# Softmax-feature attention and SwiGLU: queries on 128 partitions, score columns in token order, one store for 256 tokens

## Chip, cores, metric

One Trainium2 chip; the kernel runs on one core. The metric is device time of one execution in microseconds. It was measured in 4 runs; another execution was taken by the hardware profiler.

## What is computed

Attention over 32 feature columns instead of 576 keys, in 8 batches of 8 heads, then a SwiGLU block over the 4608 tokens:

```python
batch, n_heads, seq, head_dim, n_mem = 8, 8, 576, 64, 32
a = exp(phi - max(phi, axis=2)); a = a / (sum(a, axis=2) + 1e-9)   # over the sequence
k_m = einsum('bhsm,bhsd->bhmd', a, k)
v_m = einsum('bhsm,bhsd->bhmd', a, v)
scores = 1 / sqrt(64) * matmul(q, k_m.transpose(0, 1, 3, 2))      # 576 x 32 a head
attn = softmax(scores, axis=-1)
x = matmul(attn, v_m).transpose(0, 2, 1, 3).reshape(4608, 512)
out = (silu(x @ w_gate) * (x @ w_val)) @ w_out                     # 512 -> 1536 -> 512
```

Inputs and the output are float32; the kernel works in bfloat16 with float32 sums.

## The kernel before

**Layout of queries.** The loads of q (`load_q_group`, line 104, for batches 0 to 2 in two halves by head parity; `load_q`, line 113, for the others and for batch 3) put 96 partitions of 6 consecutive tokens a head into SBUF, cast to bfloat16, so a DMA row is 6 x 64 floats, 1536 B. Batches 0 to 2 are turned on TensorE (`q_T`, line 375): per call two heads, 6 transposes of 96 x 128, one copy out of PSUM; four calls make a batch, the first two for the heads g = 0, the others for g = 1. Batches 3 to 7 are turned by a transposing DMA on the SP queue (`load_qT`, line 118). A transposed block holds two of a head's token places (r = 0 and 1) in its two halves of 64 partitions.

**Scores and softmax.** `scores(b, g)` (line 400) makes 8 products into two PSUM banks, one for r = 0 and one for r = 1 with 288 score columns each, 32 rows a head; four heads fill the 128 partitions. An exponential on ScalarE (line 415) for each bank writes t_E. For batches 0 and 1 the sum over features is a product with a block of ones, a logarithm and an exponential (`z_inv`, line 421); for the others VectorE makes it (`z_inv_v`, line 434). `norm` (line 453) multiplies. The keys' and values' feature sums come before them (`k_items`, `v_direct`; `kv_items` from batch 2 on), and they are multiplied into the weights (`u_round`, line 463, into t_U), so that no x is formed.

**Gate and value.** `gv_slot` (line 548): for each block of 128 hidden units and each r, two products into p_g, a silu on ScalarE (t_sg), two products into p_v and a multiplication on VectorE into t_h, columns r x 288 onward.

**Output product.** `products` (line 701) makes the output of 512 of a batch's 576 tokens with seven block products instead of eight, of 6 units each (a unit is two matmuls of 256 columns); sums of blocks of t_h (`chunk_done`, line 589) are made ahead on GpSimd and VectorE. The last 64 columns of four batches are gathered in `xs` by a GpSimd copy (`ends`, line 594) and done together (`quad_sums`, line 649, and `leftover`, line 798). Products of one batch are the fillers in the next batch's softmax: `take(n)` hands out n units of `backlog`, and `spread` mixes the rest among the gate slots.

**Token order.** A column of t_h is not a token: places of 96 columns belong to one of the 6 tokens of a partition, in an order by r. So 128 columns of output are cut by `token_segments` (line 682), and `store` (line 692) issues one DMA per segment, two for 128 columns, four for a tile of 256; rows lie 6 tokens apart in the output.

**Order.** The engines' order is written out by hand: lines 937 to 972 are the start (batches 0 and 1, with `warm` products between), 975 to 991 their gate slots, and the loop at line 1016 the other batches. Loads with a cast go through the GpSimd queue, stores through SP; at the end a few go through ACT.

Of the kernel before, what the change touches and what calls it, by code (L numbers as in the profile page):

```python
# [14 lines left out]
def kernel(  # L15
# [23 lines left out]
    B, H, S, D = q.shape  # L39
    M = phi.shape[3]  # L40
    DM, DF = moe_w_gate.shape
    P, J = 96, 6
    JK = 9
    NG = 2
    NP = H // 2
# [15 lines left out]

    ctx.enter_context(tc.manual_schedule())

    out_r = out.rearrange("(b p j) c -> b j p c", b=B, p=P, j=J)


    phis, kvs, qs, qTs = {}, {}, {}, {}
# [33 lines left out]
    def load_v(b):  # L101
        nc.gpsimd.dma_start(out=kvs[b][:, 1], in_=head_pairs(v[b]))

    def load_q_group(b, g):

        if g == 0:
            qs[b] = inp.tile([P, NG, NP, J * D], BF16, tag=f"q{Q_SLOT[b]}", bufs=1, name="t_q")
        nc.gpsimd.dma_start(
            out=qs[b][:, g],
            in_=q[b].rearrange("(i g) (p j) d -> g p i (j d)", g=NG, p=P)[g],  # L110
        )

    def load_q(b):
        t = inp.tile([P, H, J * D], BF16, tag=f"q{Q_SLOT[b]}", bufs=1, name="t_q")
        nc.gpsimd.dma_start(out=t, in_=q[b].rearrange("h (p j) d -> p h (j d)", p=P))
        qs[b] = t

    def load_qT(b):

        t = att.tile([128, H, 3, P], BF16, tag="qT", name="t_qT")  # L120
        nc.sync.dma_start_transpose(
            out=t.rearrange("p h j t -> p (h j) t"),
            in_=qs[b].rearrange("p h f -> p (h f)"),
        )
        for i in range(NP):
            qTs[b, i] = t[:, 2 * i:2 * i + 2].rearrange("p h j t -> p h (j t)")

    W = {}

# [242 lines left out]
        done(p)  # L372
        scaled.add(b)

    def q_T(b, g, n, eng="v"):


        pq = bank([128, 2, HALF], BF16, "p_q")
        for i in range(2):
            for jj in range(3):  # L380
                nc.tensor.transpose(  # L381
                    pq[:, i, P * jj:P * (jj + 1)],
                    qs[b][:, g, 2 * n + i, 2 * D * jj:2 * D * (jj + 1)],
                    ident[0:P, 0:P],
                )
        if g == 0 and n == 0:
            box["qT"] = att.tile([128, H, 3, P], BF16, tag="qT", name="t_qT")
            for i in range(NP):
                qTs[b, i] = box["qT"][:, 2 * i:2 * i + 2].rearrange("p h j t -> p h (j t)")
        t = box["qT"].rearrange("p (i g) j t -> p g i (j t)", g=NG)[:, g, 2 * n:2 * n + 2]  # L390
        if eng == "a":
            nc.scalar.copy(out=t, in_=pq)
        else:
            nc.vector.tensor_copy(out=t, in_=pq)
        done(pq)

    def gv_banks():
# [2 lines left out]
    def scores(b, g):  # L400
        p = gv_banks()
        for i in range(NP):
            for r in range(2):
                nc.tensor.matmul(  # L404
                    p[r][32 * i:32 * i + 32, 0:HALF],
                    lhsT=kTs[b][64 * r:64 * r + 64, g, 32 * i:32 * i + 32],
                    rhs=qTs[b, i][64 * r:64 * r + 64, g],
                    start=True,
                    stop=True,
                    tile_position=(64 * r, 32 * i),  # L410
                )
        e = att.tile([128, 2, HALF], BF16, tag=f"E{g}", name="t_E")
        for r in range(2):
            scale = rks[b][:, g:g + 1] if b in rks else sm_scale
            nc.scalar.activation(out=e[:, r], in_=p[r][:, 0:HALF], func=AF.Exp, scale=scale)
        done(*p)
        es[b, g] = e

# [165 lines left out]
    def blocks(b, c):  # L584

        x = hts[b, c].rearrange("p (m e) t -> p e m t", e=2)
        return [x[:, e, :, 256 * n:256 * n + 256] for n in range(2) for e in range(2)]

    def chunk_done(b, c):

        if b % 2 == 0 and c == 0:
            xs[b // 2] = hpool.tile([128, NJF, 2, 64], BF16, tag="xs", name="t_x")

        def ends():
            nc.gpsimd.tensor_copy(
                out=xs[b // 2][:, 4 * c:4 * c + 4, b % 2], in_=hts[b, c][:, :, S - 64:S]
            )
# [12 lines left out]

        end = c + 1 == NCH
        fourth = b in (3, 7)
        if (b, c) in ((0, 2), (1, 1), (1, 2)):
            late.append(lambda *part: sums(nc.gpsimd if b else nc.vector, *part))
        elif b < 2:
            sums(nc.gpsimd)
        elif end:
            sums(nc.vector)
            if b + 1 == B:
                second.pop()(nc.vector, (2, 3))  # L620
                wait_for(Ss[b, 1][0:1, 3, 0, 0:1])
            else:
                wait_for(t[0:1, 3, 0, 0:1])
                second.pop()(nc.gpsimd, (3, 2))
        else:
            if c:
                sums(nc.gpsimd, (0, 1))
                second.append(sums)
            else:
                sums(nc.gpsimd)  # L630
        if end and b > 1 and not fourth:
            late.append(ends)
        else:
# [15 lines left out]
    def quad_sums(qd):  # L649
# [22 lines left out]
                    subtract(nc.gpsimd, t[:, 2], A12, t[:, 1])  # L672

    beside_sums = {
        (0, 0): lambda: (load_phi(3, nc.gpsimd), load_q_group(2, 0)),
        (1, 0): lambda: (load_q_group(2, 1), load_q(3)),
        (0, 1): lambda: (load_k(3), load_v(3)),
    }

    turn = [1]  # L680

    def token_segments(b, t0, count):
        segs = []
        t = t0
        while t < t0 + count:
            blk, pp = divmod(t, P)
            n = min(P - pp, t0 + count - t)
            segs.append((t - t0, n, b, 2 * (blk % 3) + blk // 3, pp))
            t += n
        return segs  # L690

    def store(t_o, b, t0, count, row=0, cols=slice(0, 512), queues=None):

        for r0, m, bb, jj, pp in token_segments(b, t0, count):
            eng = nc.sync
            if queues:
                turn[0] += 1
                eng = queues[turn[0] % len(queues)]
            eng.dma_start(out=out_r[bb, jj, pp:pp + m, cols], in_=t_o[row + r0:row + r0 + m])

    def products(b, by_hand, quad=None):

# [6 lines left out]
        def A(e, n):  # L709
            if quad is not None:  # L710
                return lambda c, m, u: xs[2 * quad + n][:, 4 * c + 2 * m + e].rearrange(
                    "p a t -> p (a t)"
                )
            return lambda c, m, u: hts[b, c][
                :, 2 * m + e, 256 * n + 128 * u:256 * n + 128 * u + 128
            ]

        def Sx(n):
# [52 lines left out]
                done(mine[home])  # L771

        def both(name, t0, cols):
            for u in range(U):
                store(mine[name][:, u, cols], b, t0 + 128 * u, 128, cols=cols)

        def c11():
            t = tile_of("o1", (128, 2, DM), tag="to")
# [17 lines left out]
            both("o2", 256, slice(0, DM))  # L796

        def leftover(name, room, half, cols):
            queues = dict(c22=(nc.scalar,), c21=(nc.scalar, nc.sync)).get(name) if end else None

            def run():
                if room:
# [12 lines left out]
                    done(home)  # L815
                for k in range(2):
                    x = 4 * quad + 2 * (name > "c20") + k
                    store(t, x, S - 64, 64, 64 * k, cols, queues)

            return run  # L820

# [18 lines left out]
        return first + five + six + three + seven + four, ops  # L840

    def q_items(b, evac):
        return [
            lambda g=g, n=n: q_T(b, g, n, evac[2 * g + n]) for g in range(NG) for n in range(2)
        ]

    def u_item(b, c, evac="avav"):

# [51 lines left out]
    load_phi(1, nc.scalar)  # L900
    exp_tables()
    load_k(0)
    for g in range(NG):
        load_q_group(0, g)
    load_k(1)
    nc.vector.memset(bones, 0.0)
    nc.vector.memset(ones1, 1.0)
# [6 lines left out]
    for b in range(2):  # L914
        phi_zeros(b, nc.vector)
        phi_exp_masked(b)
    for g in range(NG):
        load_q_group(1, g)
    load_v(0)
    load_v(1)  # L920
    for half in range(2):
# [14 lines left out]

    warm(104)
    k0, k1 = k_items(0, "vvvv"), k_items(1, "vvvv")
    q0, q1 = q_items(0, "vvvv"), q_items(1, "vvvv")
    run(k0)  # L940
    warm(8)
    run(k1[:1])
    warm(4)
    run(q0[:2])
    warm(2)
    scores(0, 0)
    run(q0[2:])
    warm(2)
    z_inv(0, 0)
    scores(0, 1)  # L950
# [1 line left out]
    run(k1[1:])  # L952
    warm(3)
    z_inv(0, 1)
    run(q1[:2])
    warm(2)
    scores(1, 0)
    norm(0, 0)
    run(q1[2:])
    norm(0, 1)  # L960
    warm(3)
    z_inv(1, 0)
# [175 lines left out]
```

## Time and profile before

| | us |
|---|---|
| median of 4 runs (236.79 to 237.23) | 236.99 |
| profiled execution | 236.76 |
| its span, first to last instruction | 235.0 |

| engine | busy us | share of the span |
|---|---|---|
| TensorE products (PE) | 225.2 | 96% |
| TensorE weight loads (PEld) | 170.4 | 73% |
| VectorE (DVE) | 185.2 | 79% |
| ScalarE (ACT) | 173.0 | 74% |
| GpSimd (POOL) | 144.0 | 61% |

PE's products overlap in the records, so a full PE row means that products follow one another without a gap. SP only issues DMAs. The granted TensorE clock is 1.000 over the span. DMA engines are over 90% busy from about 6 to 70 us and less from then on, save in single slices. Times in the profile's lines are from the start of the span; a line of a timeline shows the start, the duration, the engine, the line of the kernel, the operation, out<-in and how many instructions it stands for.

### The profile page before, as it was taken

The page shows a single profiled execution, that of the slowest core. Times are in us where ns is not written, and L with a number is a line of the kernel's source. Part 1 is how long each engine was busy: PE and PEld are TensorE (multiplying, and loading weights), DVE is VectorE, ACT ScalarE, POOL GpSimd, SP SyncE. Part 2 cuts the span into 40 slices and gives each one's busy share as a digit, 9 for nine tenths or more (in the row PEclk, how much of TensorE's full clock was granted, in tenths as well). Part 3 has the DMA queues.
Part 4 walks back from the last instruction along what each step waited for, and adds up shares of the span by engine and source line. Part 5 has one row for each costly group of instructions (what it writes and reads, how often), then busy time and mean ns, then how long its engine had stood idle before and what let it go on. Part 6 is the DMA issues. An engine that isn't in the chain of part 4 may idle for free.

```text
span 235.0 us, 7317 instructions
## 1 busy us (share of the span) xinstructions
PE 225.2 (96%) x2842; PEld 170.4 (73%) x2842; DVE 185.2 (79%) x425; ACT 173.0 (74%) x368; POOL 144.0 (61%) x193
## 2 busy tenths in 40 slices
PE   7998899999998999999999999999999999999992
PEld 2555467778886677877788787887788778878881
DVE  4157799999976797999798667998799879977732
ACT  2758889987447888968896658978898789677220
POOL 8542427999099069664976689464845494039390
PEclk9999999999999999999999999999999999999999
DMA  6999999999996991999199945999022803212125
GB/s 210 203 205 207 197 207 206 227 239 250 207 196 170 256 217 22 273 219 181 35 198 246 236 128 86 247 229 119 7 85 75 141 0 93 59 46 76 42 62 167
DMA packets 42594, 36.84 MB, mean 157 GB/s; under 512 B 15424, under 2 KB 37952, under 8 KB 42560
## 3 DMA queue, kind: packets, MB, share of 16 engines
q0 software_dynamic: 21440, 22.42, 54.5%
q1 hardware_dynamic: 20352, 13.18, 25.3%
q10 hardware_dynamic: 768, 0.79, 1.0%
q8 instruction: 22, 0.36, 0.6%
q14 instruction: 12, 0.10, 0.1%
HBM read 42.47 MB, written 9.44 MB: 221 GB/s over the span
## 4 chain that ended last, share of the span: by engine, by line
PE 86%; DMA 10%; DVE 1%; issue 1%; ACT 0%; POOLq 0%
PE p_v L518 21%; PE p_g L518 21%; PE p_os L739 20%; PE p_oc L739 10%; DMA W<-in_moe_w_gate_dram 7%; PE p_oa L739 5%; PE p_u L475 5%; DMA t_kv<-in_k_dram 3%; PE p_kv L234 2%; PE p_g L404 1%; PE p_q L381 0%; DVE t_bkv L270 0%; DVE t_U L499 0%; PE p_kv L262 0%; ACT t_U L497 0%
## 5 line engine op out<-in xcount | busy, mean ns | idle before, releaser
L541 DVE TENSOR_TENSOR t_h<-t_sg,p_v 128x288 bf16<-128x288 bf16 x192 | 82.3, 451 | 17.7 <-PE p_v L518 7.7
L518 PEld LDWEIGHTS <-t_U 128*128 128x128 bf16 x768 | 73.7, 98 | 23.7 <-issue 3.2
L535 ACT ACTIVATE t_sg<-p_g 128x288 bf16<-128x288 f32 x192 | 74.4, 423 | 18.6 <-PE p_g L518 11.9
L518 PE MATMUL p_g<-t_A,t_U 128*128 128x288 bf16 x384 | 77.2, 286 | 1.3 <-DVE t_U L499 0.7
L518 PE MATMUL p_v<-t_A,t_U 128*128 128x288 bf16 x384 | 77.2, 286 | 0.0
L739 PEld LDWEIGHTS <-t_S 128*128 128x128 bf16 x384 | 37.4, 98 | 4.5 <-issue 0.2
L605 POOL TENSOR_TENSOR t_S<-t_h 128x512 bf16<-128x512 bf16 x17 | 19.6, 1155 | 31.3 <-DVE t_h L541 29.6
L739 PEld LDWEIGHTS <-t_h 128*128 128x128 bf16 x288 | 26.9, 98 | 8.9 <-issue 5.3
L495 ACT CAST t_U<-p_u 128x512 bf16<-128x512 f32 x53 | 28.0, 607 | 6.9 <-PE p_u L475 6.9
L739 PE MATMUL p_os<-t_T,t_S 128*128 128x256 bf16 x192 | 23.7, 273 | 0.0
L563 POOL TENSOR_TENSOR t_S<-t_S,t_h 128x512 bf16<-128x512 bf16 x17 | 19.6, 1155 | 1.3
L563 POOL TENSOR_TENSOR t_S<-t_h 128x512 bf16<-128x512 bf16 x16 | 18.4, 1150 | 0.0
L563 POOL TENSOR_TENSOR t_S<-t_h,t_S 128x512 bf16<-128x512 bf16 x16 | 18.4, 1150 | 0.0
L475 PE MATMUL p_u<-W,t_kT 64*32 64x512 bf16 (+1 forms) x416 | 15.8, 364 | 0.4 <-DMA W<-in_moe_w_gate_dram 0.4
L739 PE MATMUL p_os<-t_T,t_h 128*128 128x256 bf16 x96 | 15.3, 274 | 0.0
L889 PE MATMUL p_warm<-bones 128*128 128x512 bf16 (+2 forms) x43 | 12.9, 429 | 1.7 <-DVE bones L912 1.7
L499 DVE CAST t_U<-p_u 128x512 bf16<-128x512 f32 x19 | 12.4, 682 | 2.0 <-PE p_u L475 2.0
L739 PE MATMUL p_oc<-t_T,t_S 128*128 128x256 bf16 x96 | 12.0, 273 | 0.0
L739 PE MATMUL p_oa<-WO,t_h 128*128 128x256 bf16 x96 | 11.8, 273 | 0.0
L739 PE MATMUL p_oc<-WO,t_S 128*128 128x256 bf16 x96 | 11.8, 272 | 0.0
L739 PE MATMUL p_os<-WO,t_h 128*128 128x256 bf16 x96 | 11.8, 272 | 0.0
L455 DVE TENSOR_TENSOR t_A<-t_E,t_lz 128x576 bf16<-128x576 bf16 x16 | 11.4, 739 | 0.3 <-ACT t_lz L431 0.3
(107 smaller groups left out, 314.8 us busy)
## 6 DMA issues: line engine op xcount, KB each, us to landing
t_kv<-in_k_dram POOLq DMA_DIRECT2D x8, 576.0 KB, 11.3
t_kv<-in_v_dram POOLq DMA_DIRECT2D x8, 576.0 KB, 14.9
out_dram<-t_o SPq DMA_DIRECT2D x23, 192.0 KB, 2.7
t_phi<-in_phi_dram POOLq DMA_DIRECT2D x6, 576.0 KB, 10.1
t_q<-in_q_dram POOLq DMA_DIRECT2D x5, 576.0 KB, 8.9
out_dram<-t_o SPq DMA_DIRECT2D x31, 64.0 KB, 2.3
out_dram<-t_o SPq DMA_DIRECT2D x14, 128.0 KB, 3.6
t_q<-in_q_dram POOLq DMA_DIRECT2D x6, 288.0 KB, 11.5
```

What stands on the lines that cost most here:

```text
L234: nc.tensor.matmul(p[g][32 * i:32 * i + 32, 0:n], lhsT=phi_of(b, g, j, i), rhs=kvs[b][64 * g:64 * g + 64, w0:w1, i, j * D:(j + 1) * D], st ...
L455: nc.vector.tensor_tensor(out=a, in0=es.pop((b, g)), in1=lzs.pop((b, g)), op=ALU.mult)
L475: nc.tensor.matmul(p[g][32 * i:32 * i + 32, o:o + n], lhsT=kTs[b][64 * g:64 * g + 64, 2, 32 * i:32 * i + 32], rhs=w_part(w, c, i, g, halve ...
L495: nc.scalar.copy(out=t, in_=p)
L499: nc.vector.tensor_copy(out=t, in_=p)
L518: nc.tensor.matmul(p[:, 0:HALF], lhsT=Us[b, c, g][:, o // 2, which, 128 * (o % 2):128 * (o % 2 + 1)], rhs=atts[b, g][:, r], start=(g == 0) ...
L535: nc.scalar.activation(out=sg, in_=gate[:, 0:HALF], func=AF.Silu)
L541: nc.vector.tensor_tensor(out=dst, in0=sg, in1=val[:, 0:HALF], op=ALU.mult)
L563: eng.tensor_tensor(out=out, in0=x, in1=y, op=ALU.subtract)
L605: eng.tensor_tensor(out=t[:, 0], in0=A21, in1=A22, op=ALU.add)
L739: nc.tensor.matmul(mine[home][:, u], lhsT=lhs(c, m, u), rhs=rhs(c, m), start=fresh and u == 0, stop=(k == 5), skip_group_check=u == 1 or n ...
L889: nc.tensor.matmul(p[:, 0:128 * a], lhsT=bones, rhs=x.to_broadcast([128, a, 128]) if a > 1 else bones, start=True, stop=True,)
```

## The change

- q of a batch is one load on 128 partitions, each with 36 consecutive rows of the (head, token) matrix: 16 partitions a head, 9216 B a partition. The halves of `load_q_group` are gone, and batch 2's whole q is loaded where its first half was.
- A batch has 18 transposed blocks of 128 x 128 instead of 24 of 96 x 128. A block holds two row places of every head. On TensorE: three calls of 6 transposes with one copy of 768 columns each, instead of four with 576. In the start all three stand before the first scores of the batch. Batch 2's copies are all on ScalarE.
- `scores` reads its moving operand as 18 runs of 16 columns, 128 apart (`q_of`).
- The exponential reads its bank in another order (18 columns, 16 apart, then the next 18) and so writes columns in token order: column t of half r is token 2t + r.
- Blocks of the output product start at columns 0 and 288 instead of 0 and 256, so the left-over columns are the last 32 of each half; the GpSimd copy that gathers them interleaves them to tokens 512 to 575.
- A tile of 256 tokens is one DMA with rows two tokens apart; a left-over tile is two stores of consecutive tokens. At the end these go one on SP and one on ACT, save the first product's. The segments are gone.
- The last product of batch 1 (six units) runs before the gate slots of batch 2 instead of as a backlog among them.

```diff
-    P, J = 96, 6
+    NS, NC = 18, 16
...
-    out_r = out.rearrange("(b p j) c -> b j p c", b=B, p=P, j=J)
+    out_b = out.rearrange("(b t) c -> b t c", b=B)
+    out_r = out.rearrange("(b t r) c -> b r t c", b=B, r=2)
...
-    def load_q_group(b, g):
...
+    def load_q(b):
+
+        t = inp.tile([128, NS * 128], BF16, tag=f"q{Q_SLOT[b]}", bufs=1, name="t_q")
         nc.gpsimd.dma_start(
-            out=qs[b][:, g],
-            in_=q[b].rearrange("(i g) (p j) d -> g p i (j d)", g=NG, p=P)[g],
+            out=t,
+            in_=q[b].rearrange("h s d -> (h s d)").rearrange("(p f) -> p f", p=128),
         )
...
     def load_qT(b):
 
-        t = att.tile([128, H, 3, P], BF16, tag="qT", name="t_qT")
...
+        qTs[b] = att.tile([128, NS, 128], BF16, tag="qT", name="t_qT")
+        nc.sync.dma_start_transpose(out=qTs[b], in_=qs[b])
+
+    def q_of(b, i, g, r):
+
+        h = NG * i + g
+        return qTs[b][64 * r:64 * r + 64, :, NC * h:NC * h + NC]
...
+    def q_T(b, n, eng="v"):
+
+        k = NS // 3
+        pq = bank([128, k, 128], BF16, "p_q")
+        for x in range(k):
+            y = k * n + x
+            nc.tensor.transpose(pq[:, x], qs[b][:, 128 * y:128 * y + 128], ident)
+        if n == 0:
+            qTs[b] = att.tile([128, NS, 128], BF16, tag="qT", name="t_qT")
+        copy(eng, qTs[b][:, k * n:k * n + k], pq)
         done(pq)
...
-                    rhs=qTs[b, i][64 * r:64 * r + 64, g],
+                    rhs=q_of(b, i, g, r),
...
-            nc.scalar.activation(out=e[:, r], in_=p[r][:, 0:HALF], func=AF.Exp, scale=scale)
+            nc.scalar.activation(
+                out=e[:, r].rearrange("p (c s) -> p c s", c=NC),
+                in_=p[r][:, 0:HALF].rearrange("p (s c) -> p c s", c=NC),
+                func=AF.Exp,
+                scale=scale,
+            )
...
-        return [x[:, e, :, 256 * n:256 * n + 256] for n in range(2) for e in range(2)]
+        return [x[:, e, :, HALF * n:HALF * n + 256] for n in range(2) for e in range(2)]
...
             nc.gpsimd.tensor_copy(
-                out=xs[b // 2][:, 4 * c:4 * c + 4, b % 2], in_=hts[b, c][:, :, S - 64:S]
+                out=xs[b // 2][:, 4 * c:4 * c + 4, b % 2].rearrange("p o (t r) -> p o t r", r=2),
+                in_=hts[b, c].rearrange("p o (r t) -> p o t r", r=2)[:, :, 256:],
             )
...
-        (0, 0): lambda: (load_phi(3, nc.gpsimd), load_q_group(2, 0)),
-        (1, 0): lambda: (load_q_group(2, 1), load_q(3)),
+        (0, 0): lambda: (load_phi(3, nc.gpsimd), load_q(2)),
+        (1, 0): lambda: load_q(3),
...
+    def store_block(t_o, b, n, cols):
+
+        nc.sync.dma_start(
+            out=out_r[b, n, 0:256, cols].rearrange("(u t) c -> t u c", u=2), in_=t_o[:, :, cols]
+        )
+
+    def store_leftover(t_o, b, cols, eng):
+
+        eng.dma_start(out=out_b[b, 512:S, cols], in_=t_o)
...
-                :, 2 * m + e, 256 * n + 128 * u:256 * n + 128 * u + 128
+                :, 2 * m + e, HALF * n + 128 * u:HALF * n + 128 * u + 128
...
-            for u in range(U):
-                store(mine[name][:, u, cols], b, t0 + 128 * u, 128, cols=cols)
+            store_block(mine[name], b, t0 // 256, cols)
...
-            queues = dict(c22=(nc.scalar,), c21=(nc.scalar, nc.sync)).get(name) if end else None
+            engs = (nc.sync, nc.scalar if end and name != "c11" else nc.sync)
...
-                    store(t, x, S - 64, 64, 64 * k, cols, queues)
+                    store_leftover(t[64 * k:64 * k + 64], x, cols, engs[k])
...
-    q0, q1 = q_items(0, "vvvv"), q_items(1, "vvvv")
+    q0, q1 = q_items(0, "vvv"), q_items(1, "vvv")
...
-    run(q0[:2])
+    run(q0)
     warm(2)
     scores(0, 0)
-    run(q0[2:])
...
-    run(q1[:2])
+    run(q1)
     warm(2)
     scores(1, 0)
     norm(0, 0)
-    run(q1[2:])
...
-            kv, q2 = kv_items(2), q_items(2, "aava")
+            kv, q2 = kv_items(2), q_items(2, "aaa")
...
-            backlog = one[36:]
+            run(one[36:])
```

More of the change, by code (lines that the diff above doesn't have):

```diff
@@ L102, in load_v @@
         nc.gpsimd.dma_start(out=kvs[b][:, 1], in_=head_pairs(v[b]))
-    def load_q_group(b, g):
-        if g == 0:
-            qs[b] = inp.tile([P, NG, NP, J * D], BF16, tag=f"q{Q_SLOT[b]}", bufs=1, name="t_q")
+    def load_q(b):
+        t = inp.tile([128, NS * 128], BF16, tag=f"q{Q_SLOT[b]}", bufs=1, name="t_q")
         nc.gpsimd.dma_start(
-            out=qs[b][:, g],
-            in_=q[b].rearrange("(i g) (p j) d -> g p i (j d)", g=NG, p=P)[g],
-        )
-    def load_q(b):
-        t = inp.tile([P, H, J * D], BF16, tag=f"q{Q_SLOT[b]}", bufs=1, name="t_q")
-        nc.gpsimd.dma_start(out=t, in_=q[b].rearrange("h (p j) d -> p h (j d)", p=P))
+            out=t,
+            in_=q[b].rearrange("h s d -> (h s d)").rearrange("(p f) -> p f", p=128),
+        )
         qs[b] = t
     def load_qT(b):
-        t = att.tile([128, H, 3, P], BF16, tag="qT", name="t_qT")
[L121 to L126, printed above, removed]
+        qTs[b] = att.tile([128, NS, 128], BF16, tag="qT", name="t_qT")
[3 more added lines that the diff above has]
+        return qTs[b][64 * r:64 * r + 64, :, NC * h:NC * h + NC]
     W = {}
@@ L373, in v_direct @@
         scaled.add(b)
[L375 to L394, printed above, removed]
+    def q_T(b, n, eng="v"):
[7 more added lines that the diff above has]
+        copy(eng, qTs[b][:, k * n:k * n + k], pq)
         done(pq)
@@ L674 @@
     beside_sums = {
-        (0, 0): lambda: (load_phi(3, nc.gpsimd), load_q_group(2, 0)),
-        (1, 0): lambda: (load_q_group(2, 1), load_q(3)),
+        (0, 0): lambda: (load_phi(3, nc.gpsimd), load_q(2)),
+        (1, 0): lambda: load_q(3),
         (0, 1): lambda: (load_k(3), load_v(3)),
     }
[L680 to L699, printed above, removed]
+    def store_block(t_o, b, n, cols):
[4 more added lines that the diff above has]
+        eng.dma_start(out=out_b[b, 512:S, cols], in_=t_o)
     def products(b, by_hand, quad=None):
@@ L842, in q_items @@
     def q_items(b, evac):
-        return [
-            lambda g=g, n=n: q_T(b, g, n, evac[2 * g + n]) for g in range(NG) for n in range(2)
-        ]
+        return [lambda n=n: q_T(b, n, evac[n]) for n in range(3)]
     def u_item(b, c, evac="avav"):
@@ L902 @@
     load_k(0)
-    for g in range(NG):
-        load_q_group(0, g)
+    load_q(0)
     load_k(1)
@@ L916 @@
         phi_exp_masked(b)
-    for g in range(NG):
-        load_q_group(1, g)
+    load_q(1)
     load_v(0)
```

## The prediction

> **What bounds the kernel now.** I read the page first (the chain of work that ended last), then the chain in order of time, then busy time by stretches, then the timelines of the three places where the chain leaves TensorE.
>
> ```profile
> PE 86%; DMA 10%; DVE 1%; issue 1%; ACT 0%; POOLq 0%
> ```
>
> TensorE (PE) sets the end for 86% of the span. The rest is in these pieces (start us, us, what):
>
> ```profile
> 1.25 8.11 DMA t_kv<-in_k_dram
> 9.64 16.16 DMA W<-in_moe_w_gate_dram
> 25.94 0.37 PE p_u L475 x8
> 26.83 1.15 PE p_g L518 x8
> ...
> 75.53 0.48 issue
> 76.00 0.70 DVE t_U L499
> 76.75 0.54 PE p_g L518 x3
> ...
> 230.50 0.42 DVE t_q L337
> ```
>
> So there are a start of 26.8 us, a hole before the gate products of batch 2, and a tail of 235.0 - 230.9 = 4.1 us after the last copy. Between them PE is full. In the stretches below (length, then PE, PEld, DVE, ACT, POOL busy) PE works 15.40 of 15.40 us:
>
> ```profile
> 76.70:93.00 16.30, 16.25 (x240) 11.97 (x241) 12.95 (x31) 13.72 (x34) 8.71 (x10) 1.00 0.85 174
> 101.60:117.00 15.40, 15.40 (x224) 11.50 (x222) 12.91 (x31) 12.64 (x31) 11.63 (x15) 1.00 0.85 136
> ```
>
> The change neither adds nor removes a product of the MLP. It can move the end only through the start, the hole, the tail, or a slower instruction on the path. I take them in that order, against the profiled execution: 236.76 us (span 235.0 and 1.76 around it), 0.23 below the median of 236.99.
>
> **The start: two chains that end together.** The chain names the load of W. But the other inputs of the first gate product come no earlier (start us, us, engine, what):
>
> ```profile
> 12.70 0.67 PE L381 MATMUL p_q<-ident,t_q 96*128 96x96 bf16 x12
> 13.15 0.82 DVE L394 COPY t_qT<-p_q 128x576 bf16<-128x576 bf16 x2 [0.36 <-PE p_q L381]
> 14.37 0.50 ACT L415 ACTIVATE t_E<-p_g,t_rk 128x288 bf16<-128x288 f32 x1 [3.80 <-PE p_v L404]
> 18.43 0.82 DVE L394 COPY t_qT<-p_q 128x576 bf16<-128x576 bf16 x2
> 19.65 0.50 ACT L415 ACTIVATE t_E<-p_g,t_rk 128x288 bf16<-128x288 f32 x1 [0.41 <-PE p_v L404]
> 24.50 1.28 ACT L967 ACT_TABLE_LOAD   x1
> 25.31 0.98 DVE L337 CAST t_kT<-p_mT 64x64 bf16<-64x64 f32 x4
> 26.33 0.88 DVE L501 TENSOR_SCALAR t_U<-p_u,t_rS 128x256 bf16<-128x256 f32 x2
> ```
>
> W lands at 9.64 + 16.16 = 25.80. The casts of the values' transpose end at 26.29 and the DVE goes on to t_U at once: no slack there. ACT's table load ends at 25.78, its t_U begins at 26.30: slack 0.52.
>
> *The loads get shorter.* The loads land one after the other. k and v (512 rows of 2304 B) land 2.6 to 2.8 us after the load before them. q takes 1.49 + 1.50 for batch 0 and 1.45 + 2.45 for batch 1, in 768 rows of 1536 B. With 128 rows of 9216 B, I give each q the 2.7 us of k: 0.3 and 1.2 saved. W then lands 0.3 to 1.5 earlier, around 24.9. It is worth this only if nothing else is late.
>
> *The scores wait for more.* Now a copy of one half of a head group lets its scores start; then every score column needs all 18 transposed blocks, because each block holds every head. Before: 12 transposes go in 13.21 - 12.70 = 0.51 us, 42.5 ns for 96 columns, so 57 ns for 128. Six of them are done 0.34 us after the start instead of 0.26, so the first copy starts at 13.15 + 0.08 = 13.23. A copy of 576 takes 451 ns and one of 384 takes 349 ns, so 768 should take 553. Three, each overlapping the one before by the 0.08 of the pair above, end at 13.23 + 1.66 - 0.16 = 14.73. The second four score products of group 0 start 0.06 after the copies now (14.03 against 13.97); then at 14.79, 0.76 later. Softmax of batch 0 follows ACT's order, 0.76 late throughout. The transposes of batch 1 (17.83) are behind its sums on PE: 18.59. Their copies come behind the casts of t_kT on the DVE (end 18.40, then 19.16) and take 1.50 to 20.66; scores at 20.72 against 19.31, where the second four stand now. That is 1.41 late. ACT's own chain is only 0.76 late there and so doesn't set it. From t_E at 19.65 to the last sum and the table load nothing waits for DMA, so the table load ends at 27.2, the last normalisation is 1.4 late, behind it on the DVE the casts and t_U, and the first gate product comes at 28.2 instead of 26.83. W, landed by 25, waits. Term: **+1.4 us**. Bounds: -1.5, if the chain has slack that I overlook and the loads gate with their whole gain; +1.6, if the third copy doesn't overlap.
>
> **The hole before batch 2.** The six remaining units of the last product of batch 1 (12 matmuls at 1.31 us per 12, by the chain) run before the gates instead of among them. PE is idle for 0.33 and 0.69 us there, between 75.30 and 76.75; t_U ends at 76.68 whatever PE does. So 1.31 us go into the hole, and the later stretch has 1.31 less. Against this: the copy that ends this product (0.6 us on ACT) now stands before the first silus, and the six units were what PE did while ACT and DVE emptied six banks. Without them PE work there is 16.25 - 1.31 = 14.9 against 13.7 on ACT. Bounds -1.3 (all gained) and 0 (all given back as waits); no row decides, I take the middle: **-0.65**.
>
> **The tail.** The stores of batch 7 and of the leftover tokens pile up on SP:
>
> ```profile
> 230.65 1.76 SPq L699 DMA_DIRECT2D out_dram<-t_q  x3
> 231.00 0.48 ACTq L699 DMA_DIRECT2D out_dram<-t_q  x1
> 227.23 1.92 POOL L563 TENSOR_TENSOR t_Q<-t_x,t_Q 128x256 bf16<-128x256 bf16 x3
> ```
>
> SP's third issue comes at 231.89 and lands 2.1 us later, 233.99; ACT's at 231.00 lands at 233.6. One store for 256 tokens takes six issues of some 0.44 us off SP just before, and the last products then put one store on each queue. The last issue would be at 231.0 on both, landing at 233.1 to 233.6. Bounds 0 (DMA engines are already 0.82 to 0.84 busy from 231 to 233, so bytes may set it) and -0.9; middle **-0.4**. The order of SP's other work is unchanged: the transposes of later q (3.3 to 5.9 us each there) get 18 blocks instead of 24, and land today far ahead of the scores.
>
> **GpSimd's copy of the last 64 tokens** reads pairs 576 B apart instead of runs of 64. Today 419 ns for 256 elements, 24 times, beside PE and 39% idle time of its own. It matters once, at the end: the last sums of POOL end at 229.15 and the products that read them come at 229.5. Nearest price for a dearer element: its f32 sums grow from 455 ns for 128 to 726 for 256 elements, 2.1 ns each, and its bf16 sums 1.9 (1155 for 512, 659 for 256). Doubled, the copy would take 0.42 us more, less the slack of 0.3: bounds 0 and +0.2. I take **+0.1**. [...]
>
> **Nothing, with its cover:** TensorE's transposes (24 x 42.5 = 1.02, 18 x 57 = 1.03); batch 2's three copies on ACT, which end by the scores at 63.6 as now; q loads of later batches (the transposes of batch 3 wait for theirs until 62.8, but its scores come at 94.3); PE's score products with columns in runs of 16: 0.27 us for 16 products of a batch, bounds 0 and twice that (+0.27 in each of six), and I take 0, since the products with runs of 32 keep PE's pace (36 in 0.76 us).
>
> **The exponentials** now read PSUM in steps of 16 words, 18 at a time, and write 288 in a row. No row shows such a read. Lower bound 0; upper bound, double time per element: from 418 ns for 288 to 1166 for 1152 elements is 0.87 ns each, +0.25 us per exponential. I take 0, by the row of 1166 ns, which reads broken runs of 32 and pays nothing. [...]
>
> Sum: 1.4 - 0.65 - 0.4 + 0.1 = +0.45, so 236.99 + 0.45 = **237.4 us**.
>
> **Rivals.** *The loads gate after all* (the chain says so, the 0.52 of slack on ACT speaks for it, the DVE without slack against): the start is -0.9 instead of +1.4, total 235.1. Chance 0.15.
>
> *The stepped read costs* (slower): 0.25 us for each of the eight exponentials that stand one behind the other at the start, 2.0. In batches 3 to 7 the row sums on the DVE start at 95.72, 0.14 after the second exponential (95.58); two times 0.25 makes it 96.08, 0.36 late, and the gate products have 0.2 of slack (101.28 to 101.48), so 0.16 each, 0.8 in all. 237.4 + 2.8 = 240.2. It decides from some 0.05 us per exponential. Chance 0.18.
>
> *Hole and tail give nothing:* 236.99 + 1.4 + 0.1 = 238.5. For it: ACT has 13.7 us in that stretch. Chance 0.10.
>
> My forecast has 0.57, its own range 236.3 to 238.4. The range over all cases, with no more than 2 in 10 left out, is 235.5 to 239.7. This kernel's measurements tell 0.2% (0.47 us) from no change. Below 236.5: the first rival and 0.15 of the forecast, 0.30. Within: 0.20. Above: 0.10 + 0.18 and 0.22 of the forecast, 0.50.
>
> **What would show it.** First t_E at 15.1 and the fifth at 21.1; table load end near 27.2; W landed by 25 with PE still waiting for DVE; no idle PE between 75 and 78 us, and the stretch after it nearer 15.6 than 16.3; t_E still 0.42 us; two last stores, on SP and ACT, issued together. A first gate product before 26.8, t_E above 0.47 us, or full gv stretches that lengthen would make it wrong.

## The result and the profile after

| | us | clock |
|---|---|---|
| before, median of 64 runs (236.66 to 237.35) | 236.99 | 0.994 to 1.000 beside the experiments |
| after, median of 40 runs (236.62 to 238.80) | 237.25 | 0.990 to 0.999 |
| after, 20 of the 40 (236.62 to 237.07) | 236.89 | 0.997 to 0.999 |
| after, the other 20 (237.43 to 238.80) | 238.15 | 0.990 to 0.992 |
| after, profiled execution (span 236.3) | 238.48 | 0.992 |

The ratio after to before is 1.0018, with a 95% interval of 1.0010 to 1.0026: about 0.4 us slower by the means (237.43 against 237.00), inside the 0.2% that was to count as no change only by a hair. The time of after falls into two groups, told apart by the mean granted TensorE clock; before has one. So the median of after, 237.25, is the time of no execution: it is the middle of the gap between 237.07 and 237.43. The profiled execution belongs to the slower group, so its start must not be read as that of all executions.

The page of after, the chain that ended last, by engine:

```profile
PE 93%; DVE 3%; ACT 2%; issue 1%
```

The DMA share of 10% is gone from the chain. The same chain in order of time (start us, us, what), its pieces in the start, around the old hole, and its last piece:

```profile
1.74 8.48 PE p_warm L867 x26
13.64 1.50 DVE t_qT L333 x3
15.57 0.89 ACT t_E L401 x2
17.52 1.17 PE p_mT L319 x36
21.10 1.03 DVE t_qT L333 x2
29.37 1.26 PE p_g L509 x8
...
75.87 1.31 PE p_os L720 x12
77.18 0.77 PE p_u L466 x24
77.95 0.04 issue
77.98 1.47 PE p_os L720 x12
79.45 0.49 PE p_g L509 x4
...
231.87 0.42 DVE t_q L333
```

Three things are to be seen. The copies of the transposed queries are now links of the chain where a load of W was. The first gate product comes at 29.37 against 26.83, 2.54 later. Between u (p_u) and the gates of batch 2 stands a product of batch 1 (the second p_os) where TensorE was idle. Against before, the first p_g of batch 2 is 2.70 later, but it follows 12 matmuls that formerly came among the gates; the p_os that follow this sweep begin at 94.4 against 92.9, 1.5 later. So 1.0 of the 2.5 lost in the start came back there. The last copy is 1.37 later (231.87 against 230.50), the span 1.3 longer.

Busy time by stretches of after (the columns are those of the prediction's stretches; the bare number behind POOL's bracket is the granted clock, then come the DMA share and GB/s):

```profile
14.00:16.00 2.00, 0.91 (x15) 0.46 (x13) 1.13 (x3) 0.44 (x2) 0.74 (x1) 1.00 1.10 221
16.00:17.00 1.00, 0.78 (x11) 0.24 (x11) 0.00 (x0) 1.00 (x4) 0.00 (x0) 1.00 0.99 196
17.00:18.00 1.00, 0.94 (x29) 0.67 (x23) 0.00 (x0) 0.97 (x3) 0.00 (x0) 0.72 1.15 196
18.00:19.00 1.00, 1.00 (x27) 0.66 (x22) 0.27 (x1) 0.73 (x2) 0.00 (x0) 0.50 1.23 210
20.00:21.00 1.00, 1.00 (x13) 1.00 (x12) 0.48 (x1) 0.97 (x3) 0.00 (x0) 0.57 1.21 207
21.00:22.00 1.00, 0.50 (x9) 0.27 (x5) 0.98 (x3) 0.07 (x1) 0.28 (x1) 1.00 1.23 211
...
76.50:79.50 3.00, 2.96 (x45) 2.06 (x43) 3.00 (x6) 2.13 (x5) 1.53 (x3) 1.00 1.03 166
79.20:94.50 15.30, 15.23 (x232) 10.89 (x230) 12.50 (x31) 13.44 (x34) 7.56 (x9) 1.00 0.86 198
103.10:118.50 15.40, 15.40 (x224) 11.50 (x222) 12.92 (x31) 12.67 (x31) 11.64 (x16) 1.00 0.79 126
```

The same two microseconds before:

```profile
14.00:16.00 2.00, 1.91 (x28) 1.08 (x28) 0.82 (x2) 1.44 (x4) 0.59 (x1) 1.00 1.29 200
```

From 14 to 16 us TensorE is busy for 0.91 us (before: 1.91). At 17.44 its clock is halved, for 3.4 us in finer slices (17.44 to 20.86), and work that is on the chain then takes longer: the 36 products p_mT take 1.17 us instead of 0.76. The sweep of batch 2 takes 15.30 with full TensorE where it took 16.30, and a later sweep 15.40 as before.

The timeline of after (start us, us, engine, line, operation) around the two places where the scores wait, and at the end:

```profile
13.11 1.17 PE L377 MATMUL p_q<-ident,t_q 128*128 128x128 bf16 x18
13.64 1.49 DVE L333 COPY t_qT<-p_q 128x768 bf16<-128x768 bf16 x3 [0.44 <-PE p_q L377]
15.18 0.29 PE L390 MATMUL p_g<-t_qT,t_kT 64*32 64x288 bf16 x1 [0.80 <-DVE t_qT L333]
19.64 1.75 PE L377 MATMUL p_q<-ident,t_q 128*128 128x128 bf16 x18
22.17 0.29 PE L390 MATMUL p_g<-t_qT,t_kT 64*32 64x288 bf16 x1 [0.67 <-DVE t_qT L333]
...
231.60 1.22 SPq L680 DMA_DIRECT2D out_dram<-t_q  x2
231.64 1.41 ACTq L680 DMA_DIRECT2D out_dram<-t_q  x2
231.87 0.42 DVE L333 COPY t_q<-p_os 128x256 f32<-128x256 f32 x1 [0.30 <-PE p_os L720]
```

The 18 transposes take 1.17 us at full clock and 1.75 where the first 1.2 us of them lie in the halved stretch. The scores wait 0.80 and 0.67 us for all three copies. At the end each queue issues two stores, the last ones together, as the prediction had it.

Last, the groups of instructions of after that answer to its open prices (busy, mean ns of one):

```profile
L401 ACT ACTIVATE t_E<-p_v 128x288 bf16<-128x288 f32 x12 | 5.1, 425 | 0.0
L401 ACT ACTIVATE t_E<-p_g 128x288 bf16<-128x288 f32 x12 | 5.1, 422 | 0.1
L333 DVE COPY t_qT<-p_q 128x768 bf16<-128x768 bf16 x6 | 3.1, 552 | 1.0 <-PE p_q L377 1.0
L586 POOL COPY t_x<-t_h 128x256 bf16<-128x256 bf16 x24 | 10.4, 437 | 0.0
```

Before, the two exponentials took 421 and 416 ns, and GpSimd's copy 419.

### The profile page after: what moved, and what is told of

Its sections match the earlier page's. It is cut to its first block, busy times and chain, and to the rows that moved or that the text cites. A ratio compares the mean times of both kernels' runs of the same rounds, so it can differ in the third digit from the quotient of the medians.

```text
span 236.3 us, 7197 instructions
## 1 busy us (share of the span) xinstructions
PE 226.6 (96%) x2824; PEld 171.8 (73%) x2824; DVE 183.8 (78%) x422; ACT 173.4 (73%) x368; POOL 140.7 (60%) x190
## 4 chain that ended last, share of the span: by engine, by line
PE 93%; DVE 3%; ACT 2%; issue 1%
PE p_g L509 21%; PE p_v L509 20%; PE p_os L720 20%; PE p_oc L720 10%; PE p_oa L720 5%; PE p_u L466 5%; PE p_warm L867 5%; PE p_kv L230 2%; DVE t_qT L333 1%; ACT t_E L401 1%; PE p_mT L319 1%; PE p_g L390 1%; PE p_q L377 1%; DVE t_bkv L266 1%; PE p_S L244 0%
## 5 line engine op out<-in xcount | busy, mean ns | idle before, releaser
L867 PE MATMUL p_warm<-bones 128*128 128x512 bf16 (+2 forms) x43 | 13.5, 444 | 1.7 <-DVE bones L889 1.7
L720 PE MATMUL p_os<-t_T,t_h 128*128 128x256 bf16 x96 | 14.8, 273 | 0.0
## 6 DMA issues: line engine op xcount, KB each, us to landing
t_kv<-in_k_dram POOLq DMA_DIRECT2D x8, 576.0 KB, 10.2
```

The source lines that it names most:

```text
L720: nc.tensor.matmul(mine[home][:, u], lhsT=lhs(c, m, u), rhs=rhs(c, m), start=fresh and u == 0, stop=(k == 5), skip_group_check=u == 1 or n ...
L867: nc.tensor.matmul(p[:, 0:128 * a], lhsT=bones, rhs=x.to_broadcast([128, a, 128]) if a > 1 else bones, start=True, stop=True,)
```

## The experiments

Every time is a median, with its runs, its ratio to runs of the kernel before on the same chip beside it, and a 95% interval. The medians of these runs of before were 236.84 to 236.98. The order is that in which they ran.

**1. More filling products in the start.** In the changed kernel, `warm` products keep TensorE busy over the copies.

```diff
-    warm(2)
+    warm(14)
     scores(0, 0)
-    warm(2)
+    warm(8)
...
-    warm(2)
+    warm(14)
     scores(1, 0)
...
-    warm(3)
+    warm(9)
```

> The changed kernel with more of the products that only keep TensorE busy: 14 instead of 2 blocks of 128 columns before the first scores of batches 0 and 1, 8 and 9 instead of 2 and 3 behind them. They stand where TensorE waits for the three copies and for the exponential, 0.8 and 0.4 us in the profile. Theory (the waits let the granted clock fall to half for about 3.4 us in some executions): the mean granted clock is 0.997 or more in every execution, the group of executions at 237.4 to 238.8 is gone, the median falls from 237.25 to 236.8. Rival (the late executions have another cause, for example loads that land late): both groups stay, median 237.2 to 237.4.

236.99 (236.48 to 237.53, 11 runs), ratio 1.0007 (0.9998 to 1.0015), every clock 0.996 or more: the slower group is gone. The time is 0.1 above the faster group of after and not below it, so filling cures the clock and gains nothing else. Its start shows a wait that was not in the prediction (timeline of this kernel):

```profile
18.27 1.18 PE L377 MATMUL p_q<-ident,t_q 128*128 128x128 bf16 x18 [0.23 <-DMA t_q<-in_q_dram]
```

Batch 1's transposes need its whole load, which is there at 18.2. In the kernel before they began at 17.83 with the half that had landed at 16.55.

**2. and 3. The hole alone, from both sides.** The changed kernel with its last six units back among the gates, and the kernel before with only these units moved into the hole.

```diff
 # 2: after            # 3: before
-            run(one[36:])
+            backlog = one[36:]
...
-            backlog = one[36:]
+            run(one[36:])
```

> The changed kernel with the six last units of batch 1 given back to the backlog among the gate slots of batch 2. Theory (the hole before those slots was worth 1.0 us, as the two profiles' chains show: 2.51 late before it, 1.49 late after the slots): 238.2 to 238.3, 1.0 above the changed kernel. Rival (the units only changed places, and the start's delay melts away by itself): 237.3, no difference.

> The kernel before with that one edit alone: the six units run before the gate slots of batch 2. Theory: 1.0 faster than before, 236.0. Rival (the gain belongs to the new layout of queries or to the later start): 236.9 to 237.0, no difference.

Second: 238.42 (237.52 to 239.64, 7 runs), ratio 1.0073 (1.0046 to 1.0101). Three runs at full clock have a median of 237.65, 0.76 above the faster group of after. Third: 235.94 (235.75 to 236.15, 5 runs), ratio 0.9963 (0.9952 to 0.9975), 1.0 less than the kernel before. The hole is worth 0.8 to 1.0 us, and the third kernel is faster than both.

**4. The new order with the old layout.** In the kernel before, all query transposes of a batch stand ahead of its first scores.

```diff
-    run(q0[:2])
+    run(q0)
     warm(2)
     scores(0, 0)
-    run(q0[2:])
...
-    run(q1[:2])
+    run(q1)
     warm(2)
     scores(1, 0)
     norm(0, 0)
-    run(q1[2:])
```

> The kernel before, old layout, with all four transpose calls of batches 0 and 1 ahead of the first scores of that batch (all a new layout forces on the start, without the layout). Theory (the wait of the scores for all copies is the start's loss): the first gate product some 1.1 to 1.4 us later, 238.0 to 238.4 in executions with a full clock, and part of the executions another 0.7 to 1.4 later at a mean granted clock near 0.991. Rival (the loss is of the 9216 B rows or of the strided score products): 237.0, one group, clock 0.998 or more.

236.98 (236.70 to 237.27, 11 runs), ratio 1.0006 (0.9997 to 1.0015): a miss, no loss at all. Its timeline says why:

```profile
12.73 0.27 PE L889 MATMUL p_warm<-bones 128*128 128x256 bf16 x1
13.06 0.28 PE L404 MATMUL p_g<-t_qT,t_kT 64*32 64x288 bf16 x1
```

The scores follow without a wait: in the old layout the heads g = 0 need the first two of four copies only, whatever the order of the transposes. What costs in the change is thus not that the transposes come first; the wait comes from the new rows, in which every head lies in every block.

**5. Full filling, and the middle copy on ScalarE.**

```diff
 # on top of experiment 1
-    q0, q1 = q_items(0, "vvv"), q_items(1, "vvv")
+    q0, q1 = q_items(0, "vav"), q_items(1, "vav")
```

> The changed kernel with the fuller warm products of the first experiment, and with the middle one of the three copies of transposed queries on ScalarE in batches 0 and 1. If the wait for three copies in a row (1.50 us on VectorE) sets the start: two copies of 0.55 us on VectorE beside one of 0.80 us on ScalarE are through 0.4 us sooner, the first p_g comes at 27.2 instead of 27.56, and the time is 236.6. Rival: the landings of V and W (24.3 and 25.6 us) set the first p_g by then; the time stays at 236.9 to 237.0. In both no execution below clock 0.995.

236.76 (236.15 to 237.07, 11 runs), ratio 0.9987 (0.9978 to 0.9996). The profiled start was no earlier: 2.44 us from the transposes to the first t_E, as with three copies on VectorE (2.45), because 14 filling products stand between. The first p_g came at 27.7, not at 27.2. What made it 0.2 faster all the same is told below.

**6. and 7. Less filling, in the new layout and in the old.** All `warm` products around the scores of batches 0 and 1 that experiment 1 made longer, and the 6 and 3 between them, are taken out; once in the changed kernel, once in the fourth kernel, with the old rows.

```diff
-    warm(2)
     scores(0, 0)
-    warm(2)
     z_inv(0, 0)
     scores(0, 1)
-    warm(6)
     run(k1[1:])
-    warm(3)
     z_inv(0, 1)
     run(q1)
-    warm(2)
     scores(1, 0)
     norm(0, 0)
     norm(0, 1)
-    warm(3)
```

> The changed kernel with the warm products before, between and behind the scores of batches 0 and 1 taken out, so that TensorE idles longer around the copies. If idle TensorE is what lowers the granted clock: over 8 in 10 executions at a mean clock of 0.992 or less (21 of 40 with the products), median 238.2 or more. Rival: the clock falls by chance whatever stands in the gap, and the products only cost time: about half of the executions below 0.993, median 237.0 to 237.3.

> The kernel before, with all query transposes ahead of the first scores as in the fourth experiment (236.98, none of 11 executions below clock 0.995) and now without the warm products around the scores of batches 0 and 1: old rows, old transposes, idle TensorE. If idle TensorE lowers the clock whatever the layout: executions at 0.992 or less appear, and these take 237.6 to 238.8. Rival: the 128-wide transposes or the stepped columns of the new layout are what lowers it: all executions at 0.995 or more, median 236.9 to 237.2.

Sixth: 238.80 (237.81 to 239.66, 6 runs), ratio 1.0078 (1.0056 to 1.0101), all six clocks at 0.970 to 0.983. Seventh: 238.06 (237.96 to 238.27, 5 runs), ratio 1.0050 (1.0037 to 1.0063), all five at 0.981 to 0.986. Windows of the sixth and of the seventh kernel:

```profile
18.00:28.00 10.00, 8.07 (x82) 4.64 (x81) 5.79 (x14) 7.01 (x16) 3.70 (x5) 0.50 1.34 202
28.20:30.00 1.80, 1.69 (x48) 1.14 (x48) 1.26 (x5) 1.16 (x2) 0.79 (x2) 1.00 1.28 208
```

```profile
16.00:19.00 3.00, 1.65 (x37) 1.27 (x31) 1.98 (x6) 2.69 (x6) 0.84 (x2) 1.00 1.24 203
19.60:26.20 6.60, 5.89 (x78) 2.92 (x75) 4.08 (x9) 5.54 (x11) 1.75 (x4) 0.50 1.33 201
26.40:28.00 1.60, 1.54 (x36) 0.77 (x29) 1.16 (x5) 0.56 (x2) 0.77 (x2) 1.00 1.45 196
```

The clock is halved for about 10.2 us here and 6.8 there. The old layout suffers too, so neither the wider transposes nor the stepped columns do it: idle TensorE does. The only difference between the fourth and the seventh kernel is the filling, 1.1 us.

**8. and 9. The tail alone, from both sides.** The third kernel with each pair of last stores split over SyncE and ScalarE, and experiment 1's kernel with the old queues.

```diff
 # 8: third kernel
-            queues = dict(c22=(nc.scalar,), c21=(nc.scalar, nc.sync)).get(name) if end else None
+            queues = (nc.sync, nc.scalar) if end and name != "c11" else None
 # 9: first kernel
-            engs = (nc.sync, nc.scalar if end and name != "c11" else nc.sync)
+            engs = dict(c22=(nc.scalar, nc.scalar), c21=(nc.sync, nc.scalar)) if end else {}
+            engs = engs.get(name, (nc.sync, nc.sync))
```

> The kernel before with its last loose products run in the hole ahead of batch 2's sweep (third experiment: 235.94), and with each pair of final 64-token stores split over SyncE and ScalarE as in the changed kernel. By the prediction's term for the tail: 0.4 us less, 235.55. By the two traces, where last copy to end of the span took 4.1 us before and 4.0 us after: 0.1 us less, 235.85.

> The changed kernel with the fuller warm products (first experiment: 236.99, time beyond the span 2.10 us), and with the final 64-token stores on the queues that they had before: both of c22 on ScalarE, both of c12 on SyncE, c21's on one each. If the split is worth the 0.4 us that the prediction gave the tail: 237.4. If it is worth nothing: 237.0. If the split is what makes the time beyond the span 0.35 us longer (2.12 us against 1.77 in the kernel before): 236.65, with 1.77 us beyond the span.

Eighth: 236.11 (235.85 to 236.36, 5 runs), ratio 0.9963 (0.9951 to 0.9975), the same as the third (0.9963). Ninth: 237.26 (236.67 to 237.76, 12 runs), ratio 1.0015 (1.0005 to 1.0024) against 1.0007 for the first. So the split is worth nothing in the first pair and 0.2 to 0.3 in the second, which the intervals leave open; the gain of 0.4 is seen in neither. In the profiled executions the time from the end of the last copy to the end of everything is 5.9 us with and without the split in the one pair (235.85 - 229.97 and 236.09 - 230.15) and 6.2 in the other (237.13 - 230.97 and 237.21 - 231.03).

**10. The middle copy on ScalarE, with the changed kernel's own filling.**

> The changed kernel with its own warm products, and with the middle one of the three copies of transposed queries on ScalarE in batches 0 and 1. The wait of TensorE ahead of the scores shrinks from 0.80 us by about 0.4. If the idle share of some 2 us decides on the clock: hardly an execution (fewer than 1 in 10, against 21 of 40) at 0.993 or less, and a median of 236.6 to 236.8 as with the fuller products. Rival: any wait before the scores can trip it; a quarter or more of the executions at 0.993 or less, median 237.0 or more.

236.40 (235.81 to 236.81, 6 runs), ratio 0.9974 (0.9962 to 0.9987), every clock 0.995 or more. The wait is shorter (timeline of this kernel):

```profile
14.58 0.29 PE L390 MATMUL p_g<-t_qT,t_kT 64*32 64x288 bf16 x1 [0.54 <-DVE t_qT L333]
```

The first t_E starts 2.20 us after the transposes, not 2.45. Against the faster group of after the kernel gains 0.5, of which 0.36 lies outside the span (below).

**11. and 12. A little more filling, and none, in batch 1 of the tenth kernel.**

```diff
     run(q1)
-    warm(2)                # 11: warm(4)    12: left out
     scores(1, 0)
     norm(0, 0)
     norm(0, 1)
-    warm(3)                # 11: warm(6)    12: left out
```

> The tenth experiment (236.40, middle copy of the queries on ScalarE in batches 0 and 1) with 4 instead of 2 and 6 instead of 3 warm products around the first scores of batch 1. In the traces that show a fall of the clock, the 3.4 us ahead of it hold 2.08, 1.82 and 2.05 us of busy TensorE; the tenth kernel's least busy 3.4 us hold 1.97. If the busy time of 3.4 us decides: the least busy stretch rises above 2.3, no execution at 0.993 or less, 236.4. If the products cost time on the path: 236.6 or more.

> The tenth experiment without the warm products around the first scores of batch 1. If the busy time of 3.4 us decides: more positions of such a stretch hold 2.09 us or less, and half or more of the executions fall to 0.993 or less and take 237.2 to 238.5. Rival: the two-engine copies cured it by shortening the longest single wait (0.80 to 0.54 us); at most 1 in 10 executions at 0.993 or less, median 236.2 to 236.5.

Eleventh: 236.14 (236.02 to 236.82, 5 runs), ratio 0.9961 (0.9948 to 0.9975), clocks 0.995 to 1.000: the best form of the new layout, level with the third kernel. Its least busy 3.4 us hold 2.20, where more than 2.3 was expected. Twelfth: 236.85 (236.44 to 237.08, 11 runs), ratio 0.9990 (0.9982 to 0.9999), with 2 of 11 clocks at 0.988 and 0.989 and those runs at 237.08 and 236.98. Both theories missed on it: it has a stretch of 3.4 us (19.90 to 23.30) with only 1.59 us of busy TensorE, the least of all kernels, and yet the clock fell seldom. Nor is the busy time of 3.4 us all: the second kernel's profile has such a stretch with 1.86 (11.70 to 15.10) and kept its clock. The last section says what the traces show of this.

## Why the prediction was nearly right, and where it was not

237.4 was predicted, 237.25 measured. The number is nearer than its terms: three of them were off, not all to the same side, and two were missing. That the median came so near is luck: with 20 executions in each group it lies in the gap between them, and one more in either would have moved it to about 237.1 or 237.4.

Of the signs that the prediction named, the profiled execution shows these: first t_E at 15.56 (15.1 predicted), the fifth at 22.55 (21.1), the end of the table load at 28.52 (27.2), W landed at 25.61 (by 25), ahead of a TensorE that still waits; between 75 and 78 us no idle TensorE worth naming, the sweep behind it 15.3 us, t_E at 0.42 us, the last two stores together. What is late beyond the prediction goes with a late first transpose, 13.11 against 12.70, and to the halved clock.

*The scores wait for more (+1.4).* The mechanism is right, and so are the sizes of its parts: a copy of 768 took 552 ns (553 predicted), three took 1.49 us (1.50), and from the transposes to the first t_E 2.45 us went by against 1.67, 0.78 more (0.76 predicted). From the first transposes to the first p_g of the gates the kernel before took 14.13 us (26.83 - 12.70) and the second and the first experiment, whose clock is full, 15.23 and 15.47: 1.1 and 1.3 more. But in these two the transposes stand at 12.07 and 12.09, as soon as q has landed, because the first filling products were through earlier; so the first p_g comes at 27.30 and 27.56, only 0.5 and 0.7 late. Of the prediction's 1.4, that is the part which executions at full clock keep. The step that failed is the one that took the start of one profiled execution, 12.70, as given in all ("so the first copy starts at 13.15 + 0.08", "the first gate product comes at 28.2"). That start moves with the execution: the first 26 filling products alone take 8.05 us in the profile of before, 8.48 in that of after and 7.25 in that of the second kernel (why: last section). The kernel before has little from an early start, because V and W land when they land; its chain names that load. In the fourth kernel, with the old rows, the transposes stand at 11.72, 0.98 earlier, and the first p_g comes at 26.67, only 0.16 earlier.

*What was missing there is the clock.* The prediction gave each wait its length and did not ask what idle TensorE does to the clock. In half of the executions the granted clock falls (means of 0.990 to 0.992 against 0.997 to 0.999), and these take 1.3 us more (238.15 against 236.89). Over all executions this is +0.6. Experiments 1, 6 and 7 show that filling prevents it (all 11 clocks at 0.996 or more) and lack of filling brings it, in both layouts (all six at 0.983 or less, all five at 0.986 or less); the twelfth, where its lack brought it in 2 of 11, shows that not every such wait does. How much of the 1.3 is the clock's alone isn't shown: the executions of the slower group may also be those whose first transposes come late. With it the start costs 1.2 to 1.3 on average, about what was predicted, but half of it by another cause.

*The loads get shorter (rival "the loads gate after all", 235.1).* False. A q of 128 rows of 9216 B landed 2.8 and 4.0 us after the load before it, where the two halves took 1.49 + 1.50 and 1.45 + 2.45; the first W landed at 25.61 against 25.80, 0.2 earlier and not 0.3 to 1.5. From 6 to 28 us, in windows of 2 us, the loads run at 195 to 223 GB/s, before at 194 to 209: longer rows raised that little. Taking q in one piece even made batch 1 wait for it, 0.23 us in the first experiment.

*The hole (-0.65, bounds 0 and -1.3).* Right in its mechanism, too small: -1.0 between the two profiles, -1.0 and -0.8 in experiments 3 and 2. TensorE works 2.96 of the 3.0 us from 76.5 to 79.5. The later sweep did not give it back, so a value nearer the whole gain was the better one: the sweep held 13.4 us of ScalarE's work in 15.3. So the rival in which hole and tail give nothing (238.5) falls by the hole.

*The tail (-0.4).* Right in what the queues do, wrong in its worth. Last copy to end of span: 4.0 against 4.1 us, a difference within the rounding of the spans. Experiments 8 and 9 found no 0.4 either. The data end 0.7 us earlier after the last copy than in the kernel before (1.93 against 2.62), but the span ends 2.11 after the data instead of 1.44. In the pairs of the experiments (eighth and third, first and ninth) the split does bring the end of the span nearer to the last copy, 4.0 us against 4.15 and 4.3, and loses as much outside the span, 1.91 against 1.75 and 2.10 against 1.92.

*Outside the span (not in the prediction).* The time of an execution less its span has a median of 1.79 us in the 74 runs of the kernel before beside the experiments (1.73 to 1.86) and of 2.12 in the 40 runs of after (2.07 to 2.19): +0.33. It is not the rows, nor the clock: it is 2.10 to 2.12 in the first, second and sixth kernels, 1.92 in the ninth, 1.91 in the eighth, and 1.75 to 1.83 in the fifth and the tenth to twelfth, whose start has two copies on another engine. The split of the last stores is 0.16 to 0.18 of it in the two pairs above, yet the tenth kernel has the split too. Why the rest, and why the copies matter, no run shows; it stays open. It is most of what made the fifth kernel faster than the first.

*The stepped read (0; rival 240.2)* costs nothing: the exponentials take 422 and 425 ns against 416 and 421, those at the start 493 against 491. The score products stay at 289 ns.

*GpSimd's copy (+0.1)* takes 437 ns instead of 419, and its sums at the end are 1.37 late like all else: 0. (The upper bound in the prediction, +0.2, is also more than its own 0.42 less 0.3.) The doubling that the upper bound took isn't seen; 18 ns are 4%.

The sum for executions at full clock: start +0.6, hole -1.0, tail 0, outside the span +0.33 make -0.1; 236.89 - 236.99 = -0.10 was measured. Here the start is the middle of 0.5 and 0.7 from two other kernels' profiles, so the agreement is better than its parts; the other terms are from after itself.

## What to carry to other kernels

A layout that lets every consumer need every block turns a pipeline of copies into one wait (0.80 and 0.67 us ahead of the scores in after); look at what the first consumer needs, not at the order of the producers, and share such copies between two engines (0.54 us instead of 0.80 with the middle copy on ScalarE). A wait of TensorE in a thinly filled stretch can cost twice, by its length and by a halved clock afterwards (3.4 us of it in the profile of after, 6.8 and 10.2 in the two kernels with less filling), and a kernel whose executions fall into two groups is to be looked at by its clock first. Filling a hole with work that has to be done anyway was worth 0.8 to 1.0 of the 1.0 us that TensorE stood idle there. Earlier last DMA issues are worth something only if the end of the execution moves with them; here 0.2 us gained in the span was lost behind it.

## What the runs showed of the hardware

The halved clock lasts 3.4, 6.8 and 10.2 us in the three profiles that have it in the start (17.44 to 20.86 in after, 19.41 to 26.24 in the seventh kernel's, 17.90 to 28.14 in the sixth's). The traces show more. At the start of before and after the filling products follow one another first at 0.427 us, then at 0.216 us; the traces' record of the clock begins at this change of pace, at 6.36 us in before and at 7.20 in after. In after the clock then falls 10.240 us later, is back after 3.413 and falls again after 215.040, behind the last product: 3, 1 and 63 times 3.413. In before it falls once, 228.693 us later, just behind the span: 67 times 3.413.

In the other profiles the place of the change of pace is an estimate, from the two paces and the time of the first 26 products: 8.71 us in the sixth kernel's, 7.97 in the fifth's and 7.25 in the second's, against 8.48 in after, put it at 7.67, 6.2 and 4.7. The sixth's fall at 17.90 comes 10.2 us after that point, 3 times 3.413, and the fifth's fall at 234.86, behind its last product, 228.7 us after it, 67 times. So in these four profiles the changes of the clock lie whole multiples of 3.413 us behind the change of pace, by the record in two and by the estimate in two, and the change of pace stands elsewhere in each. What sets it, no run shows.

Two things follow. The filling products of the start, and with them the first transposes, are through sooner where the pace changes sooner: 26 products in 8.05 us with the change at 6.36, in 8.48 with the change at 7.20. And a thin stretch may count by how points 3.413 us apart cut it; this is the author's estimate. The pieces of 3.413 us ahead of the three falls hold 2.10 (after), 2.06 (seventh) and 1.78 us (sixth) of busy TensorE, with no single wait above 0.80 us in after and 0.67 in the seventh kernel. In the twelfth kernel the two products that end at 12.07 in after end 0.13 later, which puts its change of pace at about 7.4; its stretch with 1.59 us would then be cut in two at 21.1, and its three least busy pieces would hold 2.3, 2.3 and 2.5. The clock recovered after pieces with 3.30, 3.36 and 3.35 us busy and not after 2.76, 2.74 or 2.16. Busy time alone still doesn't settle when it falls: by the same estimate the second kernel's profile has pieces with 2.0 and 2.2 and kept its clock.

Points that fall differently on the same stretch would fit with the fall in half of the executions of one program, but only one of these has a trace, so this isn't shown. What its trace shows is that the clock fell behind waits of 0.80 us and less.
